# Attention with chunk selection, then an ELU MLP: the late keys' chunk bounds by min/max trees, three engines for the rectified queries, another order of all operations

## The chip, the cores and the metric

The kernel runs on one core of a Trainium2 chip. A core has five engines with queues of their own: TensorE (PE, with its weight loads as PEld), VectorE (DVE), ScalarE (ACT), GpSimd (POOL) and SyncE (SP), which here only issues DMAs. The metric is the device time of one execution in microseconds (us), the median of several runs. Span is the stretch from the first to the last instruction of one profiled execution.

## The reference

Four batches of eight heads, 768 positions, head dimension 64. Keys lie in 24 chunks of 32. For each query an upper bound of its score with a chunk is made from the chunk's elementwise minimum and maximum; the six chunks with the highest bounds are attended.

```python
k_chunks = k.reshape(B, H, nc, chunk, D)
k_min = np.min(k_chunks, axis=3)
k_max = np.max(k_chunks, axis=3)
ub = np.sum(np.maximum(q * k_min, q * k_max), axis=-1)   # per query and chunk
ub = np.where(causal, ub, -1000000000.0)
top_chunks = np.argsort(ub, axis=-1)[..., -top_k:]
scores = scale * np.matmul(q, k.transpose(0, 1, 3, 2))
scores = np.where(mask, scores, -1000000000.0)           # selected chunk, and causal
attn = softmax(scores)
x = np.matmul(attn, v)                                   # 3072 tokens x 512
h = x @ w_in                                             # 512 x 2048
g = np.where(h > 0.0, h, np.exp(np.minimum(h, 0.0)) - 1.0)
out = g @ w_out                                          # 2048 x 512
```

## The kernel before, in words

The tokens are worked off in eight units of 384: unit 0 and 1 hold the first 192 and the next 192 positions of batches 0 and 1 (`p` and `s` in names), units 2 and 3 their second halves, units 4 to 7 the halves of batches 2 and 3. In front of each unit stands its preparation, then its selection, its attention, and after it its MLP.

Names of operations are short, and numbers behind them tell batch, half and pair of heads. What this document uses:

- `kT`, `qT`: transposes of keys and queries on TensorE (L408, L548). `kmin`, `kmax` (L372): chunk bounds of batches 0 and 1, reductions over 32 neighbouring columns out of PSUM into `kst`; `ks`: maximum minus minimum.
- Late keys are those of batches 2 and 3. `bounds_batch` loads them a second time, in another layout, as pieces `kc` of 96 rows (4 heads by 24 chunks) by 1,024 (16 positions by 64 dimensions): two pieces `y` for each batch and group of heads, eight in all. Each is reduced over its 16 positions by one strided `tensor_reduce` for the minimum and one for the maximum (L491), into `km`. `kj` (L495) joins the two pieces, `kz` (L498) subtracts, `kw` (L502) transposes on TensorE, `kv` copies into `kst`. `kb`, `ky`, `kd` make the late keys' operand of the scores: two copies and a transposing DMA (L473).
- `qt` holds transposed queries, `qr` (`relu`, L347 on ScalarE and L349 on VectorE) their positive part, `qa` the bf16 copy for the scores. With minimum m and maximum M, max(q m, q M) = q m + relu(q) (M - m), so `ub` (L603) is a product of `qt` with the minima and one of `qr` with the differences, added in PSUM.
- `ubT`, `max`, `lt`, `sT` (L614 to L631, VectorE) find each query's sixth best bound and mark the chunks below it; `mk` copies the marks into the scores' operand.
- `sc` (L785) scores, `ex` (L800, L804) exponentials on ScalarE, `tri` (L817) the triangular mask on VectorE or GpSimd, `pv` (L836) the product with the values, `rcp` and `on` (L647, L649, VectorE) the division, `xd` (L660, issued by SyncE) a transposing DMA into `xt`, for units 2 to 7.
- The MLP: `h` (L875) the first product, four matmuls for each of 16 blocks of 128; `e` (L882) the exponential on ScalarE, `m` (L884) minus one, on GpSimd or VectorE, `g` (L888, VectorE) the selection into `gT`; `o` (L899) the second product, in groups of four matmuls; `oe` its copy out of PSUM; an output store.
- The weights come in three loads `w_in0` to `w_in2` (blocks 0 to 3, 4 to 7 and 8 to 15 of `h`) and four loads `w_out`, all from GpSimd's queue. `v` casts the values to bf16 on GpSimd, ScalarE or VectorE.
- `fill` (L938): a matmul on zeros, with nothing to compute.

Nothing schedules at run time. Each operation is recorded with the engines that may take it. A string `ORDER` then lists all operations, three characters each, the first of which names the engine; a second string `PLACES` gives the buffer that each takes from the pools of `BUFS`. Operations are emitted in that order, and each engine works off its own in the order of the string, waiting on semaphores for what it reads and overwrites. Instructions of VectorE that read what VectorE has just written wait on such a semaphore too.

Of the kernel before, what the change touches and what calls it, by code (L numbers as in the profile page):

```python
# [9 lines left out]
AOT = mybir.AluOpType  # L10
AF = mybir.ActivationFunctionType
AX = mybir.AxisListType
# [6 lines left out]
D = 64  # L19
# [15 lines left out]
PE, ACT, DVE, POOL, SP = "PE", "ACT", "DVE", "POOL", "SP"  # L35
# [4 lines left out]
D01A0sS0tS0xS0XS0wA0uS2hS0YA0VG0iD00S0ZS0yS2fS0+S0vD09G0jA0rD03G0eG04PjFA0WA02P1aS2kD1bS0BP11PjG  # L40
G0aG0cP18PjIS2iPjKS2gD0-S0zP0MP0DD19D15PjHG0bA05A0QP1tP0TD0ED17A1eD1cS2QP1uP1vD1dD0kD0FD10PjMP0K
P1kA1wPjOD0HD12P1oP1pG0dS2vA0UPjJD0OD0qD06A0LG0GA0SD0lG0nP1zP1qG0fD0mD13P2oG0RPjLA1xP1hD0pPjQD0N
A1rD0oP1SG0CP1jP1RP1lA1sA16P2BD2pA1iA1nG0AP1yD2qGmjP1AA2FPjNP1XD2DA1mP1OD1TGmkP1NA1CD2rD2CS3fP2w
S2RP2JA2sP1HPjPD1PP1EA1BG07GmlD2xP1DP1ID1JP20PjSD1UA2uPjRS2PD1QP29A2KP2aPjTS2OP1YG2HG0JD1FP33P1+
S2VPjVS2mD14S2ID1KD1GA1fA2yD1ZP3gD21P1VP25D2bG2EPjUD2LA2GP1LP26D22G0PD1-D1MP23D2cD27D24A1WD28A34
P3lPjWP2dD3nD3mA36PjXD3pPjZA2eD3oD3qD3rS2TPmuD2NAmvG2AD3hG37G3sDmwPmKPmGPmOP3JG3uPmCPj+PjYPmqD2S
AmLG0IAmHP2XAmPA2tGmmDmMDmNA35PmyG08AmrGmIGmnDmxS32P38DmJPk1Pk3G3tA2+Pj-DmQPk0G3vD2YPk5Pk2A2zPk7
A3KD2ZAmzP3HD39AmDPnmS4-DmRS4YDmEPniDmFA3cGmAPm-D3aG3dPmSA3IAm+AnnGmsDmBGn0DmtP3+Pk4GnoPn6AnjPna
GnkA3iG2-Dn1DnpD3kGmoP41An7Gn8G2lAnbDnlA31A40PnDPk6PmWAmTPk8GncDn9PnwA2MPn2G3bDndP3wA42AmXGmUDmV
A2nGmYPnePnxD1gDmZPk9P4lD3yP4FS50G30A3jS4+P4DAn3G43GmpG2WPnED3AA4mGn4D3xD3zD3BD2jP4jA4EP45PnqPnr  # L50
A4GDn5D3CAnfP44G3ED46PnFD3DP3SP3QD3FG0hGngD3GPnsG3LA4kP3MG2US4ZD47S4XS7OA3RSbrSbzS57S5wP3NP4MA3T
# [12 lines left out]
D8jD8DSbADoTAptPpAA8ePpwPpoGaOG7YG8aPaPG8lG8oD88P8GD7ZApBGpCApxGpuPpcDpDSayPpgDpvGpyDpzPp0G8EApp
Pp8D8IG8bD8HAaQD8KPp4GpqDprA7-AaSApdAphGpiD8JDpjAp1PpkGpeDpfGp2G8gDp3AaTG8zD8LPpQAaRAp9SoVAp5PpI
GpaGp6ApRDpbDp7AplPpUGpSAb7A7+DpTSavPpEPpMPpYG8tPqcD8MApJSawApFSc+Pq0GpKSaCGpmDpLDpnApNGpGDpHAb9
G8NP93P8ZGcUG8OGbaSaUApZAb6ApVDp-P91Dp+PqdDpOP97DpWP96A94A92P8XG8fScLP8+DpPPq1A8-G95A8YDaWDbfA98
G99G8QP8TP8VG8PP9xP9wA90Pq2ScKP8RA8WA8UP9jP9rA9yDd0DpXP9bDaVDbhDboA8SA9kG9zP9fP9lA9sP9tP9aP9pA9m
P9hG8AA9uD9vP9nA9qDbvG8FSbBA9iDbDPq3P9RA9oP9HP9XP9WSaEGcTA9gD9cP9TP9FPqeSbbDq4D9dP9BA9YD9ZSf4A9I
DcXA9SA9GDaBP9ASazA9UP9ND9CP9PD9DP9JPahPadPa7PabSaXA9OG9VSb8A9QA9KPalP9LA9MGhxPakPqfDaZP9-DaYPaf  # L70
P9+AaePkcAbwPa3Da-Sq5ScRAa8Da+AacPkeAamDqgPq6Pa5Da0AagDa1Aa4S9EAaiSfgGb0Aa6DajGanPa9Pq7PaoAbgAaa
PapS9eSoUDbFDbdAbESa2DaqDarPb1GbGAb4Pq8Ab2PkdSasDfiAb5GbcAb3PbHDbIPq9PkfAbyDbJSbeGbiGcWDbKPkgSf5
DbLDbqDbMGcSSf9PqqPqSDbNPqmDbxAd1AqaAqrPqiAqTPquAbPGqsGbOPbYGqUAqnPbXPqCScPPreDqtDqVGqoGbRDqpPca
PbSDfhAqvDdcGqwPc9AqjAbQAbZGqkAqDGqEAbTDqlDqxPq-PqKArfDqFSf3Pr6ScNPcoPcnGrgPcCAq+AcbAr7GaDPcBDd8
PqyGr0AcpPcwSqhPr2AcDAqzPbUGr8SgbDrhDaFDr9Ar3PqWPcyDr1GcqAcxPciPqGDddGqAGr4AbVAczShkGb-Sf6Sf7PqO
Pc6ScYGcODr5AqHAqXGqIGd2AcjDqBProDd4DqJPckSgcDqYSg2Pc4ShlPraDcAAqLSfjGqMAc7ScVGbWGcEDqNPriPrjAcl
Ac5ArbDfRAd9PcFAqPAhwAd6DcmPc0GccPcrSf8PcsDc8PcGPb+Ad3DqZPceDrcPcdDd5DcHPrpGqQDqRPrqDcfDcgDrdPdg
PruPrrPrkPrlDc1GdfAfODctDc2SchGdbDcIGfPSc3DcuScvPrvScJPrIPs4PrUSqbDdiDflDdhPrASg1ArmDdkDdjSg9AfL
DdlPrwGdeSfQArsAs5DdmArVDdnPdJPdtSrnDfkSfxGrWGs6AhtPrQSfaDrXDdoPdIPrxGd7Pe6Pe7DfmArJAduGrKDs7PdF
ArBDrLAdKArRGrCGrSPrMDrDPdBDhCPdvPrESg4Ae8ArNDrOAdwArFGdqDrTDrPPsoGrGPdrPs0PsgAdCDdLPdDDryPdxAsp  # L80
AdGPdRShnAs1DrHGsqPrYSrzDsrAdsAshDe9DhuGsiPdzAdyShyDdaSgaAdEAdSPswPdVPs8ShvAdADdpDsjDdHArZGcQGs2
PdZPe1AsxPdNPdMSfXDs3GfJDr-PexAdWGsySfYDszPssDdOGfIAs9SfWPe3Ae2Dr+PdTAd-Pd+PeXDdPPeWDhEAdUPewAey
Ae0Ae4AeYPsAAstPdXPscPsBDsaPskSrtPefSfKDezAdYDfnGsuDsbDe5PeaAsdAslPeTPebGseSfeSg3PepDsfDecPelPsC
DedSfVAegPetPehDsvAemGsmGfoPfpPerAeUDsnDfsPenAeqShrPeHDfzSdQDfyDgdGfMDfZDg5AeuPsDPeJAesPeLAeoAei
GevPsMAeMAfqPejPeNPeBAeKAekPeFPeADfSPeRGg8AeOPsNAeSAeIPePDeCDeVGhAPsGGeZDeDDfbAeGPe-SeeAeQPe+PsH
PsIGfUAftDf0PsOPsJGg7Df1AgeSfuSeEDsEDfwSf2Pt2DfvPs-PtKDfrAsKGffDf-DfADfBDfCPfDPt6PsSAt3Dt4DfEAtL
As+SsLPsPGgfGtMDg6AfGAfFDf+Gt0Dt5DfHPghDt1PsWAsTGsUSfNDtNPtaPtiDsVShpAt7AsXDgiSfcPtqAtbDgjShmDgk
# [82 lines left out]
def kernel(  # L170
# [25 lines left out]
    def ap(b):  # L196
        return store[b.cls][b.slot]
# [790 lines left out]
```

## Time and profile before

| | |
|---|---|
| median of 3 runs | 288.7 us (288.42 to 289.42) |
| profiled execution | 288.57 us, its span 286.7 us |
| granted TensorE clock, mean | 0.994 |
| busy: PE / DVE / ACT / POOL | 262.3 / 225.6 / 195.9 / 148.0 us |
| bytes by DMA | 39.25 MB, 30.41 read and 6.29 written in HBM |

A row of a group shows line, engine, operation, tiles and shapes, and count; then busy time in us and the mean duration of one in ns; then the engine's idle time just ahead of such instructions and what ended it. Rows of one line or tile show shortest, median and longest duration in ns, and the first and last start. Rows of the timeline and of the chain begin with the start in us from the span's start and a length in us. Instructions of one engine overlap a little at their ends, so busy time is less than the sum of the durations. Durations of matmuls hold their way through the array; their spacing is shorter.

### The profile page before, as it was taken

Reading aid. Unit: us, or ns where it says so; the run is one execution under the profiler, and the core shown is the slowest. Engines: PE = TensorE matmul, PEld = TensorE weight load, DVE = VectorE, ACT = ScalarE, POOL = GpSimd, SP = SyncE. Lnnn points to the kernel's source line nnn. Section 1 sums busy time; section 2 is a strip of 40 time slices with the busy share of each in tenths; the row PEclk is TensorE's granted clock in tenths of the full one; section 3 lists DMA queues with packets and bytes.
Section 4 is the critical chain, followed back from the end, with each engine's and each line's share of the span. In section 5 each row is a group of like instructions: output and inputs, shape, how many; then the busy total and the mean of one; then the engine's idle time right before and its main releaser. Section 6 shows DMA issues by size and latency. Waiting matters only on the chain.

```text
span 286.7 us, 6781 instructions
## 1 busy us (share of the span) xinstructions
PE 262.3 (91%) x2373; PEld 160.9 (56%) x2404; DVE 225.6 (79%) x608; ACT 195.9 (68%) x441; POOL 148.0 (52%) x285
## 2 busy tenths in 40 slices
PE   0669899999999999998899999998999989999995
PEld 0547565585556755565455455664465446665653
DVE  0397997769999999999989999698999867631850
ACT  2167587588999866898599278973488369892631
POOL 5065389743787568965379335335486442310520
PEclk9997999999999999999999999999999999999999
DMA  8999999969994679675789569973820430013003
GB/s 153 191 200 200 205 202 225 212 134 214 200 173 143 123 154 209 89 154 162 115 188 226 105 155 203 181 127 85 182 76 2 94 74 0 16 51 116 23 1 112
DMA packets 119714, 39.25 MB, mean 137 GB/s; under 512 B 111104, under 2 KB 115456, under 8 KB 119680
## 3 DMA queue, kind: packets, MB, share of 16 engines
q1 hardware_dynamic: 113072, 33.80, 59.7%
q0 software_dynamic: 3696, 4.19, 8.5%
q10 hardware_dynamic: 2912, 0.82, 1.5%
q8 instruction: 19, 0.31, 0.5%
q14 instruction: 15, 0.12, 0.1%
HBM read 30.41 MB, written 6.29 MB: 128 GB/s over the span
## 4 chain that ended last, share of the span: by engine, by line
PE 48%; DVE 28%; DMA 9%; ACT 5%; issue 5%; POOL 2%; SPq 2%; DVEq 0%; ACTq 0%
PE bank L875 15%; PE bank L899 13%; DVE km L491 6%; PE bank L785 5%; DVE gT L888 4%; DMA xt<-on 4%; PE bank L836 3%; DMA f<-in_k_dram 3%; ACT e L882 3%; PE bank L603 2%; DVE on L649 2%; DVE kst L372 2%; PE bank L408 2%; DVE thr L622 2%; PE bank L548 2%
## 5 line engine op out<-in xcount | busy, mean ns | idle before, releaser
L875 PE MATMUL bank<-xt,w_in_sb 128*128 128x384 bf16 x512 | 92.7, 326 | 3.9 <-DMA xt<-on 2.6
L884 POOL TENSOR_SCALAR m<-e 128x384 f32<-128x384 f32 x99 | 52.7, 541 | 73.4 <-ACT e L882 57.0
L899 PE MATMUL bank<-w_out_sb,gT 128*128 128x512 bf16 x338 | 86.4, 379 | 1.8 <-issue 0.2
L882 ACT ACTIVATE e<-bank 128x384 f32<-128x384 f32 x128 | 60.4, 497 | 27.0 <-PE bank L875 22.5
L888 DVE SCALAR_TENSOR_TENSOR gT<-bank,m 128x384 bf16<-128x384 f32 x128 | 66.5, 549 | 11.1 <-POOL m L884 9.4
L800 ACT ACTIVATE pt<-bank 128x384 bf16<-128x384 f32 (+1 forms) x144 | 68.6, 551 | 4.5 <-PE bank L785 2.2
L875 PEld LDWEIGHTS <-w_in_sb 128*128 128x128 bf16 x512 | 49.1, 98 | 38.5 <-issue 6.2
L899 PEld LDWEIGHTS <-gT 128*128 128x128 bf16 x368 | 34.5, 97 | 34.7 <-issue 1.6
L785 PE MATMUL bank<-rhs,lhs 96*128 96x384 bf16 (+2 forms) x240 | 45.1, 293 | 0.4
L491 DVE TENSOR_REDUCE km<-kc 96x64 f32<-96x1024 f32 x16 | 30.5, 1918 | 0.1
L785 PEld LDWEIGHTS <-lhs 96*128 96x128 bf16 x240 | 21.9, 97 | 15.2 <-issue 1.4
L817 POOL TENSOR_TENSOR pt<-pt,tri 128x256 bf16<-128x256 bf16 (+1 forms) x24 | 21.8, 915 | 12.9 <-ACT pt L800 12.1
L325 ACT ACTIVATE o<-bank 128x512 f32<-128x512 f32 (+2 forms) x16 | 8.5, 542 | 25.5 <-PE bank L899 21.2
L372 DVE TENSOR_REDUCE kst<-bank 128x12 f32<-128x384 f32 x32 | 16.3, 541 | 11.2 <-PE bank L408 9.4
L836 PEld LDWEIGHTS <-pt 128*128 128x128 bf16 x576 | 20.9, 97 | 5.7 <-DVE pt L817 1.3
L836 PE MATMUL bank<-vext,pt 128*128 128x65 bf16 x576 | 22.7, 193 | 1.5 <-DVE pt L817 0.7
L327 POOL CAST rhs<-qt 64x384 bf16<-64x384 f32 x32 | 16.5, 519 | 10.7 <-ACT qt L325 5.8
L884 DVE TENSOR_SCALAR m<-e 128x384 f32<-128x384 f32 x29 | 13.2, 457 | 10.4 <-ACT e L882 10.2
L649 DVE TENSOR_TENSOR on<-bank,rcp 128x384 bf16<-128x384 f32 (+1 forms) x40 | 19.4, 498 | 0.8
L804 ACT ACTIVATE pt<-bank 128x512 bf16<-128x512 f32 x24 | 14.6, 617 | 0.9 <-PE bank L785 0.4
L327 POOL COPY rhs<-selT 32x384 bf16<-32x384 bf16 (+1 forms) x18 | 11.7, 651 | 5.8 <-DVE selT L631 4.9
L647 DVE RECIPROCAL rcp<-bank 128x6 f32<-128x6 f32 (+1 forms) x40 | 6.7, 179 | 9.6 <-PE bank L836 6.8
(103 smaller groups left out, 308.4 us busy)
## 6 DMA issues: line engine op xcount, KB each, us to landing
out_dram<-o SPq DMA_DIRECT2D x21, 256.0 KB, 2.3
f<-in_v_dram SPq DMA_DIRECT2D x20, 256.0 KB, 4.4
f<-in_k_dram SPq DMA_DIRECT2D x18, 256.0 KB, 4.2
fx<-in_q_dram SPq DMA_DIRECT2D x32, 96.0 KB, 3.7
kc<-in_k_dram SPq DMA_DIRECT2D x8, 384.0 KB, 4.2
w_out_sb<-in_moe_w_out_dram POOLq DMA_DIRECT2D x4, 512.0 KB, 8.4
f<-in_q_dram SPq DMA_DIRECT2D x6, 256.0 KB, 6.6
w_in_sb<-in_moe_w_in_dram POOLq DMA_DIRECT2D x2, 512.0 KB, 9.8
```

The costliest lines, as they stand in the source:

```text
L327: eng[e].tensor_copy(out=dst, in_=src)
L372: g.op(("kmin", "kmax")[w] + tag, (DVE,), lambda e, w=w, op=op: nc.vector.tensor_reduce(out=cs(w), in_=src(), axis=AX.X, op=op), reads=[(b ...
L491: nc.vector.tensor_reduce(out=ap(km)[0:96, y, w], in_=ap(kc)[0:96].rearrange("p (w d) -> p d w", d=D), axis=AX.X, op=op), reads=[(kc, 0)], ...
L649: g.op("on" + tag, (DVE,), lambda e: nc.vector.tensor_tensor(out=ap(on)[:, 0:nt].rearrange("p q h d -> p h q d"), in0=view()[:, :, :, 0:D] ...
L785: nc.tensor.matmul(ap(banks[hd])[:, o + pc:o + pc + wd], lhsT=apl(ls, G)[0:96, pr, hd, P * kb:P * (kb + 1)], rhs=ap(rs)[0:96, hd, c0 - HS ...
L800: lambda e, hd=hd, pt=pt, banks=banks, wtot=wtot: nc.scalar.activation(out=ap(pt)[:, hd, PAD:PAD + wtot], in_=ap(banks[hd])[:, 0:wtot], fu ...
L836: nc.tensor.matmul(view()[:, hd, qi, :], lhsT=ap(pt)[:, hd, P * qi + off:P * qi + off + P], rhs=ap(vx[b])[:, kb, 2 * r + hd, :], start=(kb ...
L875: nc.tensor.matmul(ap(bank)[:, 0:HS], lhsT=w_in_sb[:, kk, P * fc:P * (fc + 1)], rhs=ap(xT[i, kk]), start=(kk == 0), stop=(kk == NKK - 1))
L882: g.op(f"e{i}.{fc}", (ACT,), lambda e, eb=eb, bank=bank: nc.scalar.activation(out=ap(eb), in_=ap(bank)[:, 0:HS], func=AF.Exp), reads=[(ban ...
L884: g.op(f"m{i}.{fc}", (POOL, DVE), lambda e, eb=eb, mb=mb: eng[e].tensor_scalar(out=ap(mb), in0=ap(eb), scalar1=-1.0, scalar2=1.0, op0=AOT. ...
L888: nc.vector.scalar_tensor_tensor(out=ap(gt), in0=ap(bank)[:, 0:HS], scalar=0.0, in1=ap(mb), op0=AOT.max, op1=AOT.min),
L899: nc.tensor.matmul(ap(bank), lhsT=ap(gts[fc])[:, P * tt:P * (tt + 1)], rhs=w_out_sb[:, fc, :], start=(fc == 0), stop=(fc == NFC - 1))
```

## The change

In `bounds_batch` the two strided reductions of a piece become two trees of `tensor_tensor`. The first step of each compares the two halves of 512 columns: the minimum goes to a buffer of the pool `f` (eight of 128 by 512, otherwise used for loads), the maximum overwrites the first half of the piece. Then 256, 128 and 64 columns follow, in place, the last step into `km`. First step and remainder are operations of their own, so other work can stand between. `relu` may take GpSimd besides VectorE and ScalarE. `ORDER` and `PLACES` are replaced throughout.

```diff
--- before.py
+++ after.py
 ORDER = """
...
 PLACES = """
...
-        g.op(name, (DVE, ACT), emit, reads=reads, writes=writes)
+        g.op(name, (DVE, ACT, POOL), emit, reads=reads, writes=writes)
...
-                for w, op in enumerate((AOT.min, AOT.max)):
-                    g.op(("kmin", "kmax")[w] + f"c{tag}{y}", (DVE,), lambda e, w=w, op=op, kc=kc, y=y, km=km:
-                         nc.vector.tensor_reduce(
-                             out=ap(km)[0:96, y, w], in_=ap(kc)[0:96].rearrange("p (w d) -> p d w", d=D),
-                             axis=AX.X, op=op), reads=[(kc, 0)], writes=[(km, (w, y))])
+                t = Buf("f")
+                g.op(f"kminc{tag}{y}a", (DVE,), lambda e, t=t, kc=kc: nc.vector.tensor_tensor(
+                    out=ap(t)[0:96], in0=ap(kc)[0:96, 0:512], in1=ap(kc)[0:96, 512:1024], op=AOT.min),
+                    reads=[(kc, 0)], writes=[(t, 0)])
+                g.op(f"kmaxc{tag}{y}a", (DVE,), lambda e, kc=kc: nc.vector.tensor_tensor(
+                    out=ap(kc)[0:96, 0:512], in0=ap(kc)[0:96, 0:512], in1=ap(kc)[0:96, 512:1024], op=AOT.max),
+                    writes=[(kc, 0)])
+                for w, op, src in ((0, AOT.min, t), (1, AOT.max, kc)):
+                    def rest(e, w=w, op=op, src=src, y=y, km=km):
+                        for n in (256, 128, 64):
+                            nc.vector.tensor_tensor(
+                                out=ap(src)[0:96, 0:n] if n > 64 else ap(km)[0:96, y, w], in0=ap(src)[0:96, 0:n],
+                                in1=ap(src)[0:96, n:2 * n], op=op)
+                    g.op(("kmin", "kmax")[w] + f"c{tag}{y}b", (DVE,), rest,
+                         writes=[(src, 0), (km, (w, y))])
```

The new order holds the same 620 TensorE operations, among them 40 fills. The other engines' counts:

| operations (entries of `ORDER`) | before | after |
|---|---|---|
| VectorE | 472 | 479 (16 of them by the trees' split in two) |
| ScalarE | 446 | 438 |
| GpSimd | 256 | 272 |
| `qr` on ScalarE / VectorE / GpSimd | 17 / 11 / 0 | 6 / 6 / 16 |
| `m` on VectorE / GpSimd | 29 / 99 | 33 / 95 |
| `tri` on VectorE / GpSimd | 26 / 30 | 23 / 33 |

## The prediction

> **What bounds the kernel now.** I read the page's first part, then busy time by stretches cut at the first matmuls of the MLP units, then the chain of waits where TensorE idles.
>
> ```profile
> span 286.7 us, 6781 instructions
> PE 262.3 (91%) x2373; PEld 160.9 (56%) x2404; DVE 225.6 (79%) x608; ACT 195.9 (68%) x441; POOL 148.0 (52%) x285
> ...
> 103.83:141.42 37.59, 35.16 (x351) 20.73 (x353) 36.61 (x101) 30.00 (x74) 25.20 (x45) 1.00 0.78 152
> 231.44:262.89 31.45, 31.07 (x276) 18.94 (x281) 16.49 (x39) 24.93 (x57) 8.67 (x15) 1.00 0.14 39
> ```
>
> TensorE is the bound (262.3 of 286.7), and the change leaves its work alone: both written-out orders hold 620 TensorE operations, 40 of them the filling matmuls on zeros. So only TensorE's idle time can move. In the stretch from unit 2's first MLP matmuls to unit 3's (103.83 to 141.42; columns are length, PE, PEld, DVE, ACT, POOL) VectorE is busy 36.61 of 37.59 and TensorE idles 2.4. Where no late-key reduction runs (231.44 to 262.89) TensorE is busy 31.07 of 31.45. So VectorE holds TensorE up only while late keys are reduced. The chain shows how:
>
> ```profile
> 129.49 3.67 DVE km L491 x2
> 133.22 0.08 issue
> 133.32 0.22 DVE km L495
> 133.54 0.60 DVE o L327
> 134.28 0.56 DVE on L649
> 134.83 0.59 DVE pt L817
> 135.47 1.00 PE bank L836 x27
> 136.63 0.72 PE bank L899 x3
> 137.35 4.02 DMA xt<-on
> 141.42 2.94 PE bank L875 x17
> ```
>
> Two reductions of 1.84 each keep the last mask, divisions and output copy waiting; PV (L836) starts late, the last `on` is late, so is its transposing DMA, and unit 3's MLP waits for it:
>
> ```profile
> 135.47 1.00 PE L836 MATMUL bank<-vext,pt 128*128 128x65 bf16 x27 [0.66 <-DVE pt L817]
> ...
> 141.42 1.79 PE L875 MATMUL bank<-xt,w_in_sb 128*128 128x384 bf16 x10 [1.36 <-DMA xt<-on]
> ...
> 135.42 3.12 SPq L660 DMA_TRANSPOSE xt<-on  x2
> xt<-on SPq DMA_TRANSPOSE x24, 2.6
> ```
>
> Together 2.02 us of idle TensorE.
>
> **The tree by itself.** Eight key pieces `kc` each lose two strided reductions and get eight `tensor_tensor`: widths 512, 256, 128, 64 for the minimum and again for the maximum. None of width 512 with both inputs in SBUF and fp32 is in the trace; these rows are nearest:
>
> ```profile
> L491 DVE TENSOR_REDUCE km<-kc x16: 1842/1920/1971, 85.6 to 200.3; 96x64 f32<-96x1024 f32 x16
> L495 DVE TENSOR_TENSOR km<-km x8: 209/215/409, 99.7 to 202.8; 96x64 f32<-96x64 f32 x8
> L888 DVE SCALAR_TENSOR_TENSOR gT<-bank,m 128x384 bf16<-128x384 f32 x128 | 66.5, 549 | 11.1 <-POOL m L884 9.4
> ```
>
> From 215 ns at 64 columns to 549 at 384 is 1.04 ns a column, so 512, 256 and 128 columns take 683, 415 and 282 ns; with 215 a half costs 1,595 and a piece 3.19 us. Six of the eight wait for VectorE's own preceding result; by the 0.08 issue piece in front of L495, up to 0.5 us more. A piece is thus 3.2 to 3.7 us against 3.67 for two reductions: 0 to 0.5 gained, over eight pieces 0 to 4 us. I take 3.4, or 2 us off VectorE in all, before contention.
>
> The Trainium skill ("VectorE: DVE Perf Modes", section on the TRN2 errata) gives an fp32 tensor_tensor of N elements (N+151)/0.96 ns. By it a half would take an estimated 1,630 ns, 2% over my line. The same page (perf-mode tier table) has tensor_reduce at one element a cycle; 1,024 elements would then be some 1.2 us, and the tree a loss of 0.8 us a piece. The 1,920 ns row of this strided reduction decides against that.
>
> Contention is the unknown term. One kind of VectorE instruction stretches beside GpSimd, another doesn't:
>
> ```profile
> L884 DVE TENSOR_SCALAR m<-e x29: 341/359/1157, 34.7 to 277.0; 128x384 f32<-128x384 f32 x29
> L884 DVE TENSOR_SCALAR m<-e 128x384 f32<-128x384 f32 x29 | 13.2, 457 | 10.4 <-ACT e L882 10.2
> L817 DVE TENSOR_TENSOR pt<-pt,tri 128x512 bf16<-128x512 bf16 x13 | 6.9, 536 | 0.0
> L817 DVE TENSOR_TENSOR pt<-pt,tri x24: 259/412/887, 87.4 to 255.9; 128x512 bf16<-128x512 bf16 x13, 128x256 bf16<-128x256 bf16 x11
> L884 POOL TENSOR_SCALAR m<-e 128x384 f32<-128x384 f32 x99 | 52.7, 541 | 73.4 <-ACT e L882 57.0
> ```
>
> `m` on VectorE is 116 ns above its shortest on average (457 against 341), at worst 816; the strided reduction keeps within 1,842 and 1,971. The masks (L817, two SBUF inputs) scatter too, up to 887. The tree's 64 instructions have two SBUF inputs. L495's own excess (mean 238 to its 209) is 29 ns, `m`'s 116: the tree loses 1.9 to 7.4 us on VectorE. I take 0.07 us each, 4.5 us. Net the tree costs VectorE 2.5 us, between 2 gained and 7.4 lost: no gain by itself.
>
> **What the other moves bring.** By the two written orders, `qr` goes from 17 on ScalarE and 11 on VectorE to 6, 6 and 16 on GpSimd: five fewer on VectorE. GpSimd takes 16 times 0.54 = 8.7 us (by `m`'s row, the same shape), and has 25.20 busy of 37.59 where it is fullest.
>
> In the stretch of unit 2 the VectorE orders differ most. Besides the reductions, two `qr`, three `qa`, two `m`, two output copies and two `kst` reductions leave it:
>
> ```profile
> L349 DVE TENSOR_SCALAR qr<-qt 128x384 f32<-128x384 f32 x7 | 3.2, 457 | 0.1
> L327 DVE CAST rhs<-qt 64x384 bf16<-64x384 f32 x10 | 4.6, 457 | 0.1
> L327 DVE COPY o<-bank 128x512 f32<-128x512 f32 x10 | 6.8, 677 | 3.2 <-PE bank L899 2.6 <-DMA out_dram<-o 0.6
> L372 DVE TENSOR_REDUCE kst<-bank 128x12 f32<-128x384 f32 x32 | 16.3, 541 | 11.2 <-PE bank L408 9.4
> ```
>
> That is 7 × 0.457 + 2 × 0.677 + 2 × 0.541 = 5.6 us; two `kb`, a mask and three small ones come in, some 2 us by the rows above (0.54 for the mask, under 0.5 for each other). Five reductions there (9.6 us) become five first steps and five remainders, 2.5 pieces at 3.4 plus contention of 20 × 0.07, 9.9. The stretch loses 3.3 us of VectorE work out of 36.61 and has slack again. Ahead of the last two divisions stand one remainder, two `kj` and one `qt`, some 2 us, in place of the 3.67 of two whole reductions, the output copy, a mask and two copies; and the four transposing DMAs of that unit follow each other on SyncE, where before a load and an output store stood between them. From the last PV to unit 3's first MLP matmul the new order keeps twelve L899 matmuls (2.9 us at 0.24 each, from the 0.72 of three), a selection product and a key transpose (0.8 together by the gaps around them in the old order); the last transposed tile needs a reciprocal and division (0.7) and a landing of 2.6, at worst 4.02. So between no wait and one of 1.0 is left. Of the 2.02 I take 1.5 gained (0 to 2.4).
>
> Later, unit 5's MLP:
>
> ```profile
> 203.29 0.30 PE L502 MATMUL bank<-ident_f,km 96*128 96x96 f32 x1 [0.64 <-DVE km L498]
> ```
>
> TensorE waits 0.64 there for the last two reductions, queued behind the last `on`. Now only one remainder (about 1 us), two `kj` and a subtraction stand behind it, with four L899 groups to cover: 0.5 gained. Unit 4's stretch gets half a piece more (1.8 us with contention) and loses four masks (0.54 at most each): a draw.
>
> **What doesn't move.** The start hangs on the weights, and GpSimd's queue issues them:
>
> ```profile
> 20.94 1.75 POOL L295 DMA_DIRECT2D w_in_sb<-in_moe_w_in_dram  x2
> 22.94 0.76 POOL L295 DMA_DIRECT2D w_in_sb<-in_moe_w_in_dram  x1
> DMA to landing us min/median/max: 8.6/11.0/16.1
> 37.98 0.93 PE L938 MATMUL bank<-zeros 128*128 128x256 bf16 x7
> 39.12 2.77 PE L875 MATMUL bank<-xt,w_in_sb 128*128 128x384 bf16 x16
> ```
>
> The third load lands 16.1 after 22.94, at 39.04, and at 39.12 the first block that needs it runs, after seven fills. The new order brings scores and PV of the first units earlier, but that block still waits for the load, with 0.9 us more real work done by then (18.3 us of it before, 19.2 now, counting each operation by its spacing on PE). The load is now issued behind three small key steps and two copies: up to 2 us later by their order, though the queues ahead of it hold the same bytes. Between 0.9 gained and 1.1 lost: I take 0.2 gained. Unit 6's MLP waits for its DMA as before, with 4.3 us of cover in place of 5.0: 0.2 lost.
>
> **Sum.** -1.5 - 0.5 - 0.2 + 0.2 = -2.0 against the profiled execution's 288.57 (span 286.7 and 1.9 around it). That execution is 0.13 under the median 288.7, which gives 286.7.
>
> **Rivals.** *The tree and GpSimd get in each other's way* (slower). GpSimd is busy 67% of the fullest stretch; an instruction that finds it in the middle of a 0.54 us one waits 0.27, so 0.18 on average. Sixty-four of them are 11.6 us: about 1.4 a piece, two pieces in the stretch of unit 1, two and a half in that of unit 2, three in that of unit 4. Unit 1's, which keeps two pieces and gets two more `kst` reductions and some copies on VectorE, goes over its TensorE work by about 1, unit 4's by 1.5, and GpSimd's later `m` (for which `gT` waits 9.4 us already) adds some 1; less 0.5 of the gains, about 3 over the median, 291. It decides from about 0.15 us a tree instruction. For it: the 1,157. Against it: L495's median 215.
> The Trainium skill ("SBUF — State Buffer", section on SBUF's two separate sides) states it as a lock: a VectorE instruction with two SBUF inputs and a GpSimd one that reads SBUF exclude each other for the whole instruction. The 341 to 1,157 of `m` agrees.
>
> *Nothing measurable.* The new order swaps the old stalls for as many new ones, or the third weight load comes 1 to 2 us later and eats the gain: 288.7 within 0.3% (0.87 us, about what a measurement of this kernel can tell from no change). For it: the stalls shown are accidents of a few tenths, and every queue is reordered.
>
> *More than forecast.* Unit 2's stretch loses all of its 2.4, unit 5's its 0.64, units 3 and 4 another 0.5 from fewer masks on VectorE, and the start gains its 0.9: -4.5, 284.2.
>
> **How the numbers follow.** Forecast and the better case together 0.53, no change 0.20, slower 0.27 (contention 0.17, a late third load with a new stall in the middle 0.10, some 290). The range goes from the better case, 284.2, to 290.6, just under the contention case.
>
> **What would show it.** Right: TensorE's idle time between units 2 and 3 under 1.2 us, VectorE under 34 us there, no wait for `km` at L502's successor; the 512-wide steps near 0.69 with a tail, the first block on the third load near 39. Wrong: 512-wide steps averaging over 0.85, longer `m` on GpSimd and more of `gT`'s wait on it, or that first block starting after 40.

## The result and the profile after

| | us, median (lowest to highest) | runs | against the kernel before [95% interval] |
|---|---|---|---|
| before | 288.73 | 4 | |
| after | 298.22 (296.57 to 299.16) | 4 | 1.0319 [1.0266, 1.0372] |

The change costs 9.5 us. The profiled execution of the changed kernel took 297.64 us, span 295.8. First the head of its page: the span, busy time of each engine, and the clock granted to TensorE in 40 slices.

```profile
span 295.8 us, 6867 instructions
PE 268.0 (91%) x2404; PEld 162.8 (55%) x2404; DVE 234.7 (79%) x647; ACT 195.9 (66%) x434; POOL 170.2 (58%) x301
...
PEclk9999999999999999999699999999999999999999
```

VectorE went from 225.6 to 234.7 us, GpSimd from 148.0 to 170.2, and TensorE, whose work is the same, from 262.3 to 268.0. Part of TensorE's rise is only in the records (the row of before counts 2,373 matmuls, that of after 2,404), and part is a half clock: the 6 in the row of the clock stands near 140 us; the page of before shows a lower digit only in its fourth slice, near 22.

Next, busy time by stretches (length; PE, PEld, DVE, ACT, POOL; clock; DMA share and GB/s). The first row is the stretch of unit 1 before; then, of after, that of unit 1, that of unit 2 up to the end of the wait for unit 3's tile, as the prediction cut it, and a short one.

```profile
66.90:103.70 36.80, 35.94 (x337) 22.12 (x339) 34.81 (x84) 32.27 (x76) 24.38 (x64) 1.00 0.81 162
```

```profile
65.80:108.70 42.90, 38.25 (x346) 22.91 (x344) 40.10 (x103) 31.70 (x71) 30.79 (x46) 1.00 0.65 139
108.70:151.90 43.20, 37.93 (x353) 22.15 (x352) 38.03 (x109) 30.79 (x71) 31.02 (x48) 0.92 0.69 146
139.40:146.20 6.80, 5.75 (x62) 3.95 (x61) 4.14 (x11) 2.65 (x6) 5.02 (x8) 0.50 0.43 101
```

Unit 1's stretch grew by 6.1 us, and unit 2's from 37.59 to 43.20, by 5.6; what follows from unit 4's MLP on (178.2) is 2.8 us shorter than its counterpart, since some of its work now stands earlier. In unit 1's, VectorE is busy 40.10 of 42.90, and TensorE idles 4.65 us instead of 0.86. In the last row TensorE has half its clock for 6.8 us.

The tree's steps are not what they were taken to be. Groups by form (busy us, mean ns), then one view with shortest, median and longest (ns):

```profile
L494 DVE TENSOR_TENSOR kc<-kc 96x512 f32<-96x512 f32 x8 | 6.5, 809 | 0.1
L500 DVE TENSOR_TENSOR kc<-kc 96x256 f32<-96x256 f32 x8 | 6.3, 782 | 0.0
L491 DVE TENSOR_TENSOR f<-kc 96x512 f32<-96x512 f32 x8 | 5.8, 725 | 0.0
L500 DVE TENSOR_TENSOR kc<-kc 96x128 f32<-96x128 f32 x8 | 4.5, 569 | 0.3
L500 DVE TENSOR_TENSOR f<-f 96x256 f32<-96x256 f32 x8 | 4.1, 516 | 0.0
L500 DVE TENSOR_TENSOR f<-f 96x128 f32<-96x128 f32 x8 | 4.1, 513 | 0.3
L500 DVE TENSOR_TENSOR km<-kc 96x64 f32<-96x64 f32 x8 | 3.7, 462 | 0.3
L500 DVE TENSOR_TENSOR km<-f 96x64 f32<-96x64 f32 x8 | 3.6, 453 | 0.3
L828 DVE TENSOR_TENSOR pt<-pt,tri 128x512 bf16<-128x512 bf16 x7 | 5.4, 770 | 1.6 <-ACT pt L811 1.6
L350 POOL TENSOR_SCALAR qr<-qt 128x384 f32<-128x384 f32 x9 | 11.0, 1226 | 3.1 <-ACT qt L326 2.8
L350 POOL TENSOR_SCALAR qr<-qt 128x192 f32<-128x192 f32 x7 | 5.7, 817 | 1.6 <-DVE qt L594 1.6
L899 DVE SCALAR_TENSOR_TENSOR gT<-bank,m 128x384 bf16<-128x384 f32 x128 | 65.8, 546 | 15.1 <-POOL m L895 14.3
```

```profile
L500 DVE TENSOR_TENSOR kc<-kc x16: 288/510/2300, 89.0 to 210.1; 96x256 f32<-96x256 f32 x8, 96x128 f32<-96x128 f32 x8
```

The eight tree rows add up to 38.6 us; the 16 reductions that they replace had 16 × 1.92 = 30.7. A step of 256 columns averages 782 ns in one group and 516 in the other, and one step took 2,300. VectorE's masks of 512 columns grew too, from 536 to 770 ns, and `gT` waits 14.3 us for GpSimd's `m` instead of 9.4. But both are as large in a_whole below, which has the new order without the trees and loses nothing (750 ns and 15.2 us), so they are not what costs the time. What stood beside the step of 2,300 ns shows in two timelines, VectorE's and GpSimd's (start, us):

```profile
88.98 2.62 DVE L500 TENSOR_TENSOR kc<-kc 96x256 f32<-96x256 f32 x2
```

```profile
88.46 0.85 POOL L328 CAST rhs<-qt 64x384 bf16<-64x384 f32 x1
89.28 1.14 POOL L828 TENSOR_TENSOR pt<-pt,tri 128x512 bf16<-128x512 bf16 x1
90.40 0.61 POOL L339 TENSOR_SCALAR vext<-f 128x512 bf16<-128x512 f32 x1
```

Two steps together take 2.62 us from 88.98 on, 2.30 of it one step: it starts while GpSimd reads SBUF, and ends 0.27 us after the third of GpSimd's instructions, which ends at 91.01. TensorE pays for it. Its own timeline, with what ended each wait:

```profile
93.15 0.81 PE L796 MATMUL bank<-rhs,lhs 96*128 96x384 bf16 x4 [3.02 <-DVE o L328]
...
138.98 0.49 PE L796 MATMUL bank<-rhs,lhs 96*128 96x384 bf16 x2 [1.82 <-DVE on L660]
...
140.62 0.84 PE L847 MATMUL bank<-vext,pt 128*128 128x65 bf16 x12 [1.05 <-DVE pt L828]
...
143.25 1.91 PE L910 MATMUL bank<-w_out_sb,gT 128*128 128x512 bf16 x4
...
151.90 1.30 PE L886 MATMUL bank<-xt,w_in_sb 128*128 128x384 bf16 x7 [1.17 <-DMA xt<-on]
```

The wait ahead of unit 3's MLP for a transposed tile is still there (1.17, before 1.36), and larger ones have come ahead of it. The chain of waits names what stands before the division that ends the wait of 1.82:

```profile
135.98 0.66 DVE kc L500
136.66 1.12 DVE kc L500
137.87 0.51 issue
138.38 0.54 DVE on L660
138.93 1.64 DVE pt L828
```

Steps of the tree hold up a division, just as whole reductions did before. The mask behind it takes 1.64 us by itself (408 ns on average where GpSimd reads nothing, see b_still), and the next product with the values waits for it.

### The profile page after: what moved, and what is told of

It reads as the page before. It is cut to its first block, busy times and chain, and to the rows that moved or that the text cites. A ratio compares the mean times of both kernels' runs of the same rounds, so it can differ in the third digit from the quotient of the medians.

```text
span 295.8 us, 6867 instructions
## 1 busy us (share of the span) xinstructions
PE 268.0 (91%) x2404; PEld 162.8 (55%) x2404; DVE 234.7 (79%) x647; ACT 195.9 (66%) x434; POOL 170.2 (58%) x301
## 4 chain that ended last, share of the span: by engine, by line
PE 44%; DVE 36%; issue 6%; DMA 5%; POOL 4%; ACT 4%; ACTq 0%; DVEq 0%; POOLq 0%
PE bank L886 15%; PE bank L910 13%; DVE gT L899 7%; PE bank L796 4%; DMA f<-in_k_dram 4%; DVE kc L500 4%; PE bank L847 3%; DVE f L500 2%; DVE pt L828 2%; DVE on L660 2%; PE bank L409 2%; DVE km L500 2%; DVE thr L633 2%; DVE qt L594 2%; PE bank L614 2%
## 5 line engine op out<-in xcount | busy, mean ns | idle before, releaser
L910 PE MATMUL bank<-w_out_sb,gT 128*128 128x512 bf16 x368 | 90.8, 382 | 0.2
L895 POOL TENSOR_SCALAR m<-e 128x384 f32<-128x384 f32 x95 | 49.8, 534 | 59.7 <-ACT e L893 42.1
L899 DVE SCALAR_TENSOR_TENSOR gT<-bank,m 128x384 bf16<-128x384 f32 x128 | 65.8, 546 | 15.1 <-POOL m L895 14.3
L828 POOL TENSOR_TENSOR pt<-pt,tri 128x512 bf16<-128x512 bf16 (+1 forms) x30 | 29.2, 983 | 12.3 <-ACT pt L815 6.6
L796 PEld LDWEIGHTS <-lhs 96*128 96x128 bf16 x240 | 22.1, 98 | 21.8 <-issue 6.6
L847 PE MATMUL bank<-vext,pt 128*128 128x65 bf16 x576 | 24.6, 198 | 4.1 <-DVE on L660 1.6
L847 PEld LDWEIGHTS <-pt 128*128 128x128 bf16 x576 | 22.8, 101 | 9.9 <-issue 2.7
L326 ACT ACTIVATE o<-bank 128x512 f32<-128x512 f32 (+1 forms) x16 | 8.7, 556 | 23.1 <-PE bank L910 19.7
L328 POOL COPY rhs<-selT 32x768 bf16<-32x768 bf16 (+1 forms) x16 | 12.5, 782 | 15.6 <-DVE selT L642 14.8
L350 POOL TENSOR_SCALAR qr<-qt 128x384 f32<-128x384 f32 (+1 forms) x16 | 16.7, 1047 | 4.7 <-ACT qt L326 2.8
L895 DVE TENSOR_SCALAR m<-e 128x384 f32<-128x384 f32 x33 | 15.5, 474 | 4.0 <-ACT e L893 3.7
L828 DVE TENSOR_TENSOR pt<-pt,tri 128x256 bf16<-128x256 bf16 (+1 forms) x18 | 11.1, 624 | 6.2 <-ACT pt L815 4.5
```

The lines of the kernel that those rows point to most:

```text
L328: eng[e].tensor_copy(out=dst, in_=src)
L796: nc.tensor.matmul(ap(banks[hd])[:, o + pc:o + pc + wd], lhsT=apl(ls, G)[0:96, pr, hd, P * kb:P * (kb + 1)], rhs=ap(rs)[0:96, hd, c0 - HS ...
L828: eng[e].tensor_tensor(out=view, in0=view, in1=tri[:, 64:64 + P].rearrange("p (a b w) -> p a b w", a=1, b=1) .to_broadcast([P, 2, len(dg), ...
L847: nc.tensor.matmul(view()[:, hd, qi, :], lhsT=ap(pt)[:, hd, P * qi + off:P * qi + off + P], rhs=ap(vx[b])[:, kb, 2 * r + hd, :], start=(kb ...
L895: g.op(f"m{i}.{fc}", (POOL, DVE), lambda e, eb=eb, mb=mb: eng[e].tensor_scalar(out=ap(mb), in0=ap(eb), scalar1=-1.0, scalar2=1.0, op0=AOT. ...
L899: nc.vector.scalar_tensor_tensor(out=ap(gt), in0=ap(bank)[:, 0:HS], scalar=0.0, in1=ap(mb), op0=AOT.max, op1=AOT.min),
```

## The experiments

Three theories. *Contention*: VectorE's instructions with two SBUF inputs and GpSimd's that read SBUF hold each other up. *Price of the rectified query*: GpSimd takes over 1.2 us for one of 128x384, so it falls behind. *Order*: the new order is worse, whatever the operations cost. All ratios are to runs of the kernel before on the same chip (median 289.03, 289.12 and 289.64 us in three groups).

| kernel | order | bounds of late keys | us | ratio [95% interval] |
|---|---|---|---|---|
| a_relu_two | new | tree | 298.63 | 1.0319 [1.0274, 1.0364] |
| a_whole | new | reductions | 287.94 | 0.9959 [0.9936, 0.9983] |
| a_whole_two | new | reductions | 290.29 | 1.0037 [1.0014, 1.0061] |
| b_tree | old | tree | 294.64 | 1.0184 [1.0129, 1.0239] |
| b_tree_mix | old | tree, alternating | 298.05 | 1.0340 [1.0287, 1.0393] |
| a_order | new | reductions, `qr` not on GpSimd | 289.87 | 1.0024 [1.0006, 1.0043] |
| b_still | old | reductions, GpSimd reads nothing | 284.18 | 0.9821 [0.9802, 0.9840] |
| b_tree_still | old | tree, GpSimd reads nothing | 283.53 | 0.9796 [0.9763, 0.9829] |
| a_still | new | tree, GpSimd reads nothing | 281.62 | 0.9721 [0.9660, 0.9782] |
| a_busy | new | tree, TensorE filled at two waits | 294.79 | 1.0169 [1.0107, 1.0231] |
| a_relu_act | new | tree, `qr` not on GpSimd | 297.93 | 1.0289 [1.0214, 1.0364] |
| a_half | new | one step, then reduction | 288.53 | 0.9967 [0.9932, 1.0001] |

Of the ranges that were expected, a_whole_two, a_still and a_busy miss theirs by under 0.5 us; larger misses are named below.

### Which part of the change costs the time

**a_whole** takes the changed kernel and puts back the two strided reductions, the minimum's in place of the first step:

```diff
-nc.vector.tensor_tensor(out=ap(t)[0:96], in0=ap(kc)[0:96, 0:512], in1=ap(kc)[0:96, 512:1024], op=AOT.min)
+nc.vector.tensor_reduce(out=km[0:96, y, 0], in_=ap(kc)[0:96].rearrange("p (w d) -> p d w", d=D), axis=AX.X, op=AOT.min)
...
-nc.vector.tensor_tensor(...)   # the three remainder steps of the maximum
+nc.vector.tensor_reduce(out=km[0:96, y, 1], in_=ap(kc)[0:96].rearrange("p (w d) -> p d w", d=D), axis=AX.X, op=AOT.max)
```

> The changed kernel with each tree's place taken by the one strided reduction of before (minimum where the first minimum step stood, maximum where the maximum's remainder stood), order and rectifications as changed. Theory B: 290 to 293, and VectorE's busy time falls by about 8 us. Theory A: 295 to 297, since the rectifications stay. Theory C: 296 to 298.

**b_tree** does the reverse: the old order, with four steps of a tree in place of each reduction, in a scratch laid over early constants.

```diff
-nc.vector.tensor_reduce(out=ap(km)[0:96, y, w], in_=ap(kc)[0:96].rearrange("p (w d) -> p d w", d=D), axis=AX.X, op=op)
+nc.vector.tensor_tensor(out=t[0:96], in0=ap(kc)[0:96, 0:512], in1=ap(kc)[0:96, 512:1024], op=op)
+for n in (256, 128, 64):
+    nc.vector.tensor_tensor(out=t[0:96, 0:n] if n > 64 else ap(km)[0:96, y, w], in0=t[0:96, 0:n], in1=t[0:96, n:2 * n], op=op)
```

> The kernel before in its old order, with each strided reduction replaced where it stands by the four tensor_tensor of a tree (scratch in space that the early constants have left free). Theory B: VectorE's key work grows from 30.5 to some 36 us or more and the time to 291 to 295. Theory A and C: within 1 us of the kernel before.

287.94 and 294.64: the new order with reductions is 0.4% faster than before (0.2 to 0.6%), the old order with trees 1.8% slower. The loss is the tree's, and the theory of the order falls. The tree costs 5.6 us in the old order and 10.3 in the new; a_whole came out 2 us better than any theory expected. With a_half, below, it is the fastest of the kernels that leave nothing out, though by only some 1 us.

With the order held fixed, the stretches of units 1 and 2 show where the trees cost the time. In a_whole:

```profile
66.80:106.70 39.90, 37.83 (x341) 22.89 (x345) 36.62 (x90) 31.62 (x72) 28.88 (x43) 1.00 0.69 150
106.70:143.30 36.60, 34.27 (x346) 20.18 (x349) 32.72 (x81) 30.12 (x70) 30.60 (x51) 1.00 0.77 163
```

The trees lengthen unit 1's stretch from 39.90 to 42.90, by 3.0 us, and unit 2's, up to its next MLP matmul at 150.1, from 36.60 to 41.40, by 4.8, the half clock included; the later ones differ by at most 0.3. The other half of unit 1's growth against the kernel before is the new order, which is shorter further on (in a_whole 117.0 us from unit 4's MLP on, before 120.4).

### What a rectified query on GpSimd is worth

**a_order** leaves the reductions of a_whole and gives the 16 `qr` of GpSimd to ScalarE in the written order; **a_relu_act** does the same to the changed kernel, with its trees.

> The new order alone: strided reductions as before, and the 16 rectifications that went to GpSimd run on ScalarE at the same places of the order. Theory that GpSimd's slow rectification (1.16 us) still costs something in the version with strided reductions (287.9): 285.5 to 287.5. Theory that it is hidden there: 287.5 to 289.

> The changed kernel with trees, the 16 rectified queries on ScalarE instead of GpSimd, in the same places of the order. With strided reductions this move cost 1.9 us (287.94 to 289.87). Contention theory: 16 GpSimd instructions of 0.8 to 1.2 us no longer hold up the trees, so the steps get shorter (512 wide under 750 on average) and it is 293 to 297. If the price of the rectified query on GpSimd mattered most: under 292. If neither, costs add: 300.

289.87 against 287.94, and 297.93 against 298.22. 289.87 lies above both ranges that were expected, and 297.93 between contention's (up to 297) and the 300 of neither theory. Taking `qr` off GpSimd gains nothing with trees and loses 1.9 us with reductions. In a_relu_act the steps of the tree add up to 39.8 us, with GpSimd at 153.7 us instead of 170.2: it was not the long `qr` that held them up, and the 750 ns expected for its 512-wide steps were not met (816 and 718 in the two groups). The theory of the price falls. GpSimd's price was misjudged all the same, as the profile after showed.

Whether the price comes from the form with one operation was tried with two, in the changed kernel (**a_relu_two**) and in a_whole (**a_whole_two**):

```diff
-eng[e].tensor_scalar(out=dst(), in0=src(), scalar1=0.0, scalar2=None, op0=AOT.max)
+eng[e].tensor_scalar(out=dst(), in0=src(), scalar1=0.0, scalar2=1.0, op0=AOT.max, op1=AOT.mult)
```

> The changed kernel, with the rectification on GpSimd and VectorE written with two operations (max with 0, then times 1) like the minus-one step m, and nothing else touched. Theory A (the 16 rectifications on GpSimd cost 1.16 us each instead of the planned 0.54, and hold GpSimd and VectorE up): they fall to about 0.55 us and the time to 291 to 294. Theory B (the trees' 64 two-input instructions and GpSimd block each other): the time stays above 295. Theory C (the new order is bad by itself): it stays above 296.

> Both together: the changed kernel with strided reductions and with the two-operation rectification. If A and B carry the loss between them: 286 to 290, at or near the kernel before. Theory C: 294 or more, as the order stays.

The group of `qr` on GpSimd in a_relu_two:

```profile
L350 POOL TENSOR_SCALAR qr<-qt 128x384 f32<-128x384 f32 x9 | 13.8, 1533 | 2.7 <-ACT qt L326 2.3
```

1,533 instead of 1,226 ns, where 550 was expected: the second operation adds 307. `m` has two operations (add, multiply) on the same shape and takes 541 before. By these rows it is the maximum that is dear on GpSimd; why is left open. It changed the time little with trees (298.63) and by 2.4 us with reductions (290.29 against 287.94).

### Contention, taken away

**b_still** is the kernel before, **b_tree_still** the kernel b_tree, with each GpSimd instruction that reads SBUF replaced by one that only writes a constant over the same output. The diff of the most frequent one, `m`; the others alike:

```diff
-eng[e].tensor_scalar(out=ap(mb), in0=ap(eb), scalar1=-1.0, scalar2=1.0, op0=AOT.add, op1=AOT.mult)
+eng[e].memset(ap(mb), 0.0) if e == POOL else eng[e].tensor_scalar(out=ap(mb), in0=ap(eb), scalar1=-1.0, scalar2=1.0, op0=AOT.add, op1=AOT.mult)
```

> The kernel before, with the reading operations of GpSimd (casts, copies, masks, m, ks, kz) replaced by memsets of the same output, so that GpSimd reads nothing; that part of the computation is left out. It is the base for the next kernel. Contention theory: VectorE's masks and m, which had a long tail beside GpSimd, lose most of it; time 285 to 289. Otherwise 288 to 289.

> The same kernel without GpSimd reads, with trees in place of the strided reductions. Contention theory (the trees lose their time to GpSimd reading at the same moment): the 512-wide step falls from 836 ns to under 700, the key work on VectorE below 28 us, and the time is within 1 us of the kernel without GpSimd reads or below it. Latency theory (each step waits for the one before, and the queue behind it): the steps stay long or the time stays 3 us or more above it.

The steps by form, first in b_tree, then in b_tree_still (`early` is the scratch; the last row of the first view gives shortest, median and longest):

```profile
L494 DVE TENSOR_TENSOR early<-kc 96x512 f32<-96x512 f32 x16 | 13.4, 836 | 0.2
L496 DVE TENSOR_TENSOR early<-early 96x256 f32<-96x256 f32 x16 | 8.0, 503 | 0.6
L496 DVE TENSOR_TENSOR early<-early 96x128 f32<-96x128 f32 x16 | 6.5, 406 | 0.5
L496 DVE TENSOR_TENSOR km<-early 96x64 f32<-96x64 f32 x16 | 5.5, 344 | 0.7
L496 DVE TENSOR_TENSOR km<-early x16: 220/222/1064, 88.9 to 209.8; 96x64 f32<-96x64 f32 x16
```

```profile
L495 DVE TENSOR_TENSOR early<-kc 96x512 f32<-96x512 f32 x16 | 10.8, 677 | 0.2
L497 DVE TENSOR_TENSOR early<-early 96x256 f32<-96x256 f32 x16 | 6.7, 421 | 0.5
L497 DVE TENSOR_TENSOR early<-early 96x128 f32<-96x128 f32 x16 | 4.6, 287 | 0.5
L497 DVE TENSOR_TENSOR km<-early 96x64 f32<-96x64 f32 x16 | 3.5, 221 | 0.7
```

33.4 us (36 or more were expected of b_tree) become 25.6, and the sign turns: with GpSimd's reads the tree loses 5.6 us (294.64 against 289.03), without them it gains 0.65 (283.53 against 284.18, with intervals that overlap). The strided reduction does not care; its row in b_still:

```profile
L492 DVE TENSOR_REDUCE km<-kc 96x64 f32<-96x1024 f32 x16 | 30.4, 1917 | 0.1
L823 DVE TENSOR_TENSOR pt<-pt,tri 128x512 bf16<-128x512 bf16 x13 | 5.3, 408 | 0.4 <-ACT pt L803 0.3
```

1,917 ns there, 1,918 before. The 512-wide mask, with two SBUF inputs, goes from 536 to 408. The time of b_still itself, 284.18, is below all that was expected. GpSimd is also less busy in these kernels, since writing alone is shorter (`m` 431 ns instead of 541). b_still carries that part too, so the pair tells of the tree alone.

**a_still** does it to the changed kernel, whose `qr` on GpSimd also only write:

> The changed kernel, trees and new order as they are, but every GpSimd instruction that reads SBUF (m, masks, rectified queries, subtractions, casts) only writes a constant over the same output; this part of the computation is left out. To be held against the kernel before with the same left out (284.18). Contention theory: steps at 670 to 700 (512 wide) and 410 to 430 (256), no halved clock after 30 us, no long waits for VectorE in the middle, 282 to 284. If the loss comes from the trees' own length or from the new order, it stays: some 9 us over 284, 290 or more.

```profile
L498 DVE TENSOR_TENSOR kc<-kc 96x512 f32<-96x512 f32 x8 | 5.5, 683 | 0.1
L495 DVE TENSOR_TENSOR f<-kc 96x512 f32<-96x512 f32 x8 | 5.3, 668 | 0.0
L504 DVE TENSOR_TENSOR km<-kc x8: 220/220/222, 89.3 to 195.6; 96x64 f32<-96x64 f32 x8
```

281.62 us, 2.6 less than b_still, with ratios whose intervals lie apart: without GpSimd's reads the whole change is a gain of 2.6 us; with them it loses 9.5. The eight groups of steps add up to 25.4 us instead of 38.6, 13.2 less, or 0.21 us for each of 64 instructions. So the loss goes away as a whole, and not in part.

GpSimd is busy for 114.9 us in a_still and 170.2 in the changed kernel, so its shorter time could be the cause and not the missing reads. The traces, step by step, speak against that. In the changed kernel 32 of the 64 steps take over 0.03 us more than in a_still, and each of these starts while a GpSimd instruction that reads SBUF is running (six others start so too and lose nothing). In a_still 32 steps as well start while a GpSimd instruction is running, but one that only writes, and none of them is longer for it: the 64-wide steps, which reach 1,064 ns in b_tree, all take 220 to 222.

The same count tells why the new order loses more. In b_tree 19 of 64 steps are held up, 7.8 us in all; in the changed kernel 32, 13.2 us. One that is held up loses 0.41 us in both. In the new order more steps meet a reading instruction; which of its changes brings that about, no run separates.

The Trainium skill ("SBUF — State Buffer", section on SBUF's two separate sides) says that a VectorE instruction with two SBUF inputs and a GpSimd one exclude each other only if the latter reads SBUF, and that the one that starts first holds off the other for its whole length. The pairs above agree: 836 against 677 ns at 512 columns, and 1,918 against 1,917 for the reduction, which has one input.

### Dependent steps

**b_tree_mix** puts the steps of minimum and maximum alternately, so that no step waits for the result just ahead of it; all of a piece runs at the place of the first reduction.

```diff
+for n in (512, 256, 128, 64):
+    for v, op in enumerate((AOT.min, AOT.max)):
+        a = ap(kc) if n == 512 else src[v]
+        nc.vector.tensor_tensor(out=src[v][0:96, 0:n] if n > 64 else ap(km)[0:96, y, v], in0=a[0:96, 0:n], in1=a[0:96, n:2 * n], op=op)
```

> The old order with trees, minimum and maximum steps of a piece taken in turn at the place of the first of the two reductions, so that a step hardly waits for its own predecessor. Latency theory: the time falls from 294.6 to 290 to 292. Contention theory: it stays at 293 to 296.

298.05, 3.4 us more than b_tree and above both ranges. The steps add up to 33.2 us, as in b_tree (33.4), and the idle time ahead of them falls from 2.0 to 0.3. The gaps between dependent steps are not where the time went; b_tree_still has them too, and loses nothing. All eight steps of a piece now stand together, though, so this kernel also moved the second tree ahead; what that costs is not shown. Part of the 3.4 will be the next subject: this kernel has TensorE at half clock for 6.8 us from 131.7 on, b_tree for 3.4 from 129.5.

### The clock after a wait

**a_busy** fills TensorE's time at the two waits of the changed kernel at 136 to 141 us with 18 matmuls on zeros, written where the real product follows:

```diff
 def score(...):
+    for _ in range(10 if (tag, si, hd) == ("112", 2, 0) else 0):
+        nc.tensor.matmul(ap(banks[hd])[:, 0:256], lhsT=zeros[:, 0:P], rhs=zeros, start=True, stop=True)
 def pv(...):
+    for _ in range(8 if (tag, hd) == ("112", 1) else 0):
+        nc.tensor.matmul(ap(o3)[:, 0:256], lhsT=zeros[:, 0:P], rhs=zeros, start=True, stop=True)
```

> The changed kernel with 18 more matmuls on zeros (0.11 us each at full clock) put ahead of the two waits between 136 and 141 us, 10 in front of one score product and 8 in front of one PV product, in PSUM that the real product then writes. If the halved clock after these waits costs time of its own: granted clock 1.00 from 126 on, the four L910 matmuls after the stall at 1.03 and not 1.91, and 295.0 to 296.5. If the halved stretch hides behind VectorE, which is late anyway: 297.7 to 299, with or without the halving.

The stretch of 3.40 us that holds the wait of 1.82, in the changed kernel (the 6.80 us behind it, at half clock, stand above), and then both stretches in a_busy:

```profile
136.00:139.40 3.40, 1.57 (x12) 0.74 (x9) 3.33 (x5) 2.06 (x5) 3.40 (x6) 1.00 0.25 41
```

```profile
136.00:139.40 3.40, 2.66 (x19) 1.81 (x19) 3.33 (x5) 2.02 (x6) 3.40 (x6) 1.00 0.23 48
139.40:146.20 6.80, 6.51 (x107) 4.41 (x114) 6.15 (x15) 3.36 (x10) 4.90 (x8) 1.00 0.46 106
```

More work on TensorE, and 3.4 us less time: 294.79, with a ratio whose interval lies apart from that of the changed kernel. The clock stays at 1.00, the waits for the division and the mask end at the same time as before (138.76 instead of 138.98, 140.41 instead of 140.62), and from there to unit 3's first MLP matmul it takes 7.1 us instead of 9.5 (147.47 and 150.08); the wait of 1.17 that follows in the changed kernel is gone, too. So a third of the loss, 3.4 of 9.5 us, is the clock, as a consequence of the waits; by the ratios, each of which compares with the kernel before on the same chip, it is 1.5 of 3.2 per cent, nearly a half. The four executions of the changed kernel point the same way: 296.57 and 297.64 us at a mean granted clock of 0.988, 298.79 at 0.982 and 299.16 at 0.977.

The Trainium skill ("TensorE: Matmul & The Clock Gate", Part 1, the HAM clock gate) has the array fall to half its clock after at least one idle window of about 3.4 us. The lengths here, 3.4 and 6.8, fit such a window; idle it need not be, since TensorE was busy for 1.57 us of the 3.40 ahead of the halving.

### Fewer instructions with two inputs

**a_half** keeps the first step of each tree and reduces the remaining eight positions in one strided instruction: 16 instructions with two SBUF inputs instead of 64.

```diff
-for n in (256, 128, 64):
-    nc.vector.tensor_tensor(out=ap(src)[0:96, 0:n] if n > 64 else ap(km)[0:96, y, w], in0=ap(src)[0:96, 0:n], in1=ap(src)[0:96, n:2 * n], op=op)
+nc.vector.tensor_reduce(out=ap(km)[0:96, y, w], axis=AX.X, op=op, in_=ap(src)[0:96, 0:512].rearrange("p (w d) -> p d w", d=D))
```

> The changed kernel with the first step of each tree (512 wide) kept and the rest as one strided reduction of 8 positions: 16 instructions with two SBUF inputs instead of 64. By the strided reduction's 1.92 us for 16 positions the rest takes some 0.9 to 1.05 us, a half some 1.75 to 1.85 us, 28 to 30 us in all, against 38.6 in the changed kernel and 30.5 for whole reductions. Contention theory: loss in proportion to instructions with two SBUF inputs, 287.5 to 290.5. If the 512-wide steps at these places in the order carry the loss: 293 or more.

```profile
L499 DVE TENSOR_REDUCE km<-kc 96x64 f32<-96x512 f32 x8 | 8.3, 1041 | 0.0
L491 DVE TENSOR_TENSOR f<-kc 96x512 f32<-96x512 f32 x8 | 6.7, 839 | 0.0
```

288.53, about as a_whole: the first steps are as long as in the changed kernel (839 and 776 on average, 725 and 809 there), but there are only these 16, and with the reductions (1,041 and 1,026) all comes to 29.4 us. So the 512-wide steps at these places do not carry the loss; taking the other 48 away removes it. The rows of the changed kernel and of a_still say the same: of the 13.2 us the 16 first steps have 1.5, the other 48 steps 11.7.

## Why the prediction was wrong, step by step

- **Contention, the step that failed.** "I take 0.07 us each, 4.5 us" was 13.2 us, 0.21 each; the upper bound of 7.4 was too low as well. It was bounded by `m` on VectorE, which has one SBUF input, so that its 341 to 1,157 ns are no evidence for a lock between instructions with two and GpSimd, as the prediction took them; and by the 64-wide `kj`. The nearest row was the 512-wide mask, which has two: 536 ns on average, and 408 without GpSimd's reads. That excess, 0.13 us, is what b_tree's steps show in the old order ((33.4 - 25.6) / 64 = 0.12); the 256-wide masks lose less, 327 against 285. In the new order it is 0.21, since half of the steps are held up and not 19 of 64, with `qr` on GpSimd or without (a_relu_act: 29 held up, 39.8 us of steps). A mean excess taken from one place in an order did not carry over to another.
- **The signs of being wrong** did not show it. The 512-wide steps were to average over 0.85 us; they took 0.73 and 0.81. `m` on GpSimd grew no longer (534 ns), and `gT`'s longer wait for it is in a_whole, too. The loss sat in the narrow steps: 453 and 462 ns at 64 columns, instead of 220.
- **The stretch of unit 2.** VectorE was to lose 3.3 us and get slack; the stretch takes 43.20 us, VectorE is busy 38.03 in it, where it was to be under 34, and TensorE's idle time, to be under 1.2, is 5.3 against 2.4. Unit 1's stretch, in which the forecast counted no loss, has VectorE at 40.10 us; it grew by 6.1 us, half of it by the order and half by the trees.
- **The tree by itself** was right: 683, 415, 282 and 215 ns were estimated, 668 to 683, 400 to 421, 287 and 221 measured without GpSimd's reads; 25.5 us for 64 steps, and 25.4. The line was drawn through a row of another kind (L888, with one input in PSUM), so some luck is in how well it fits.
- **`qr` on GpSimd** at 0.54 us was wrong: 1.23 us for the nine of `m`'s shape, a factor of 2.3, and 0.82 for the seven of half the width, 16.7 in all instead of 8.7. The shape was that of `m`, the operation another. It cost nothing of the result, as a_order and a_relu_act show.
- **The start.** The load was read rightly: the third load of `w_in` is issued later, at 25.37, and lands 13.1 us after that, at 38.5; its first block runs at 38.66. Unit 1 starts its MLP at 65.80 instead of 66.90, 1.1 us earlier, where 0.2 and at most 0.9 was forecast. That this is a gain of the order is not shown: the trace of before has TensorE at half clock from 21.8 to 25.2 us, that of after not, and a_whole and a_half, which begin like the changed kernel but with such a half clock, start unit 1's MLP at 66.83 and 66.91.
- **Unit 5's wait for `km`** (0.64) is gone, as forecast:

```profile
L513 PE MATMUL bank<-ident_f,km 96*128 96x96 f32 x4 | 1.1, 268 | 0.1
```

- **The sum.** The -2.0 counted gains alone, and took the trees' net cost on VectorE as hidden in its slack. The order with reductions gave -1.1 (a_whole), and the whole change -2.6 where GpSimd reads nothing (a_still against b_still). That the latter is near -2.0 is in part luck: those kernels lack a good part of GpSimd's work.
- **The rival of contention** had the mechanism and nearly the price (0.18 us an instruction, 11.6 in all), but 291 as its time, 7 us short (its own terms, 3 over 288.7, make 291.7). It counted what VectorE goes over in each stretch and took the rest as hidden. Two things were missing. VectorE had little slack in the stretches of units 1 and 2 to hide it: between unit 0's MLP and the end TensorE idles 17.1 us instead of 12.1. And those waits brought a halved clock, 3.4 us, which is in no part of the prediction. The chance of 0.17 for it was too low for a change that puts 64 instructions of the very kind that scattered in the trace beside an engine that is half busy and then gets more work.

## What to carry to other kernels

Price an added instruction by its row at places where the neighbouring engine is busy, and take the row of the same kind (number of SBUF inputs), not of the same size. Where one can be held up, ask how many will be, and for how long: here it was 19 or 32 of 64, at 0.41 us each; a shorter sum of shortest times can be a longer sum of means. A slow instruction that nothing holds up, such as a strided reduction with one input, may beat four fast ones that GpSimd can block. When TensorE gets new waits of 2 to 3 us, look at the granted clock behind them before accounting for the loss, and fill such waits if they must stay.

## What the runs showed of the hardware that was not expected

- **Half clock in the middle of a kernel.** All halvings that end before the kernel does last 3.4 or 6.8 us. Those after 30 us follow a stretch of 3.4 us in which TensorE was busy for little of it: 1.57 us in the changed kernel, 1.04 in a_relu_two, 1.26 in b_tree, 0.00 in b_tree_mix, 0.88 and 0.63 ahead of the two in a_relu_act. A wait that is split between two such stretches did nothing: that of 3.02 us which ends at 93.15 in the changed kernel left 1.93 and 1.85 us of work in the two, and the clock stayed at 1.00. In a_relu_two a like wait fell into one stretch:

```profile
89.70:93.10 3.40, 1.04 (x30) 0.82 (x27) 3.32 (x6) 1.64 (x4) 1.93 (x3) 1.00 0.02 5
93.10:99.90 6.80, 5.91 (x43) 3.92 (x44) 4.29 (x12) 3.15 (x7) 0.00 (x0) 0.50 0.64 164
```

  One stretch of a_busy with 1.48 us of work was not followed by a halving, so busy time alone isn't the whole rule; what else belongs to it is left open.
- **A maximum on GpSimd** takes 1,226 ns for 128x384 in fp32 with one operation and 1,533 with two, an add with a multiply 541.
- **The kernel before is 4.9 us faster without GpSimd's reads**, too: 284.18 with constants written in their place, against 289.12. How much of that is the reads and how much GpSimd's shorter time is not shown.
